# A linear-attention block gated by a mixer: another table of shifts for the scheduler

## The chip, the cores and the metric

The kernel runs on one core of one Trainium2 chip. The metric is the device time of one execution in microseconds (us), the median of the runs. The core has five engines that work from queues of their own: TensorE (PE: matmuls; its weight loads are PEld), VectorE (DVE), ScalarE (ACT), GpSimd (POOL) and SyncE (SP), which here issues transfers. A transfer (DMA) is issued by SP or by POOL; POOL's add to what is already at the destination.

## The reference

```python
def reference(A_x, A_wqkv, A_wo, B_x, B_w1, B_w2, B_w3, B_w4):
    def _A_ref(x, wqkv, wo):
        B, S, D = x.shape
        H = 32; Dh = D // H
        qkv = (lambda x, *d: x.transpose(*d))((x @ wqkv).reshape(B, S, 3, H, Dh), 2, 0, 3, 1, 4)
        q, k, v = qkv[0], qkv[1], qkv[2]
        phi = lambda t: jnp.where(t > 0, t + 1, jnp.exp(t)) + 1e-6
        pq, pk = phi(q), phi(k)
        kv = jnp.einsum("bhsd,bhse->bhde", pk, v)
        z = jnp.einsum("bhsd->bhd", pk)
        num = jnp.einsum("bhqd,bhde->bhqe", pq, kv)
        den = jnp.einsum("bhqd,bhd->bhq", pq, z)[..., None] + 1e-6
        o = num / den
        return (lambda x, *d: x.transpose(*d))(o, 0, 2, 1, 3).reshape(B, S, D) @ wo

    def _B_ref(x, w1, w2, w3, w4):
        h = _gelu(_layernorm(x, axis=-1) @ w1)
...
        hs = jnp.concatenate([g0, g1, g2, g3], axis=-1) @ w2
        x1 = x + hs
        h2 = _gelu(_layernorm(x1, axis=-1) @ w3) @ w4
        return x1 + h2

    x = A_x
    xn = _layernorm(x, axis=-1)
    s = _A_ref(xn, A_wqkv, A_wo)
    g = _silu(_B_ref(xn, B_w1, B_w2, B_w3, B_w4))
    return x + s * g
```

g0 to g3 are the four quarters of h's columns, shifted by +1, -1, +2 and -2 rows. x has 2048 rows of 512 columns, all in f32; the weights are 512 x 1536 (wqkv), 512 x 512 (wo, w1, w2), 512 x 1376 (w3) and 1376 x 512 (w4).

## The kernel before

The rows are worked in sixteen tiles of 128 (i) and four blocks of 512 (b, four tiles each). An f32 operand is split into a high and a low part (names that end in h and l), and a product is made of three matmuls: high by high, low by high, high by low. Many products are further cut into halves on each side and put together from seven smaller products (names s1 to s4 and t1 to t4 are the sums that this takes; a, b, e in pa, pb, pe name the PSUM bank, p1, p5, u2 the partial results that ACT brings out of a bank).

In order of time: the start loads wk and the transposed first block of x (tiles wk_s, xt), splits them into wk_0h, wk_0l and so on and u_0h, u_0l and so on (ACT makes the high parts, DVE the low parts, and DVE sums the weight's chunks into wkt), and makes the keys k. Then come, for all blocks, queries, keys, the 512 x 512 product g of phi(k) and xn, the first mixer product h and the second one; from about 230 us the MLP's first product for block after block (`up_late`), with the attention sums put in between (`attends`: so collects the result, pas, pbs, pes are its banks), and from about 410 us the MLP's second product (`down_late`) for blocks 2, 3 and 1. In `down_late` the results are collected in xo, POOL adds x1 from memory to it by a transfer (xo<-x1d), ACT makes silu of it (th<-xo), DVE multiplies by the attention's result (so, or sb where that comes back from memory), POOL adds x, and SP stores th to out.

Nothing of the order is written out by hand. Each call (`mm`, `act`, `tt`, `stt`, `fetch`, `gather`, ...) only adds an operation to a list, with its engine, an estimate of how long it is busy, and what it reads and writes; the rows of the profile that show L146, L168, L191 and so on are such helpers. `deadlines` (L243) gives each operation a due time, backwards from the time at which PE is expected to need its result. `nudged` (L237) then takes pairs (n, k) from the table and moves the due time of the n-th operation of the list earlier by a quarter of k microseconds (later for a negative k), and `backward` (L279) passes earlier due times on to what feeds it. `emit` (L285) plays all engines forward: it takes for each engine the operations whose inputs are there and for which a buffer is free, and issues of those that can start soonest the one with the earliest due time. So a shift of one due time moves an operation in its engine's queue, and what follows from it in the buffers moves others. Each engine works its queue strictly in the order written here. PSUM has four banks for groups of matmuls (tag mm) and four for the long sums (tag acc): a group can begin when ACT or DVE has read the bank's last content.

The change touches the table `SOONER` (from L1828) alone, in the function that builds the kernel; L1895 hands it to `emit`.

Of the kernel before, what the change touches and what calls it, by code (L numbers as in the profile page):

```python
# [411 lines left out]
def linear_attn_gated_by_mixer(  # L412
# [1401 lines left out]
    for b in LINE:  # L1814
# [14 lines left out]
        25, 43, 34, 17, 48, 11, 52, 22, 57, 4, 63, 3, 76, 3, 88, -164, 90, 14, 91, -77, 94, 30, 95, 2, 96, 3,  # L1829
        97, 30, 98, -40, 100, -16, 103, 30, 105, -42, 112, 38, 115, -66, 118, -34, 124, 73, 125, 16, 129, 1,  # L1830
        147, 3, 150, 6, 151, -80, 176, 20, 207, 16, 216, 3, 233, 11, 234, 29, 248, 17, 252, 3, 259, 25, 261, 42,
        262, 18, 275, 8, 282, -131, 283, -49, 302, 83, 314, -14, 315, 24, 316, 21, 321, 25, 326, 6, 331, 17,
        336, -29, 341, -44, 354, 27, 355, -45, 375, 27, 405, -6, 406, -36, 410, -76, 415, 40, 416, -23, 424, 11,
        427, 23, 428, -30, 433, -9, 434, -77, 435, 22, 443, 67, 445, -24, 451, 7, 454, -24, 456, 18, 478, 13,
        485, -8, 488, -69, 489, -119, 491, -65, 492, -3, 504, 30, 522, 77, 532, -9, 542, -1, 544, 5, 545, 15,
        552, 36, 553, -28, 563, -29, 568, -26, 571, -22, 586, 29, 591, 24, 600, -25, 616, 11, 618, 10, 627, -50,
        631, 22, 650, 6, 654, -53, 657, -29, 660, 9, 676, 8, 678, 7, 688, -19, 694, -22, 704, -15, 705, 19, 710,
        -18, 713, 22, 714, 15, 717, -23, 721, -22, 724, 36, 726, -14, 728, 7, 733, 5, 761, 17, 797, 13, 806, 36,
        807, -10, 814, -15, 815, -38, 827, 85, 844, 20, 847, 3, 849, -51, 862, -35, 867, -36, 870, -19, 873, 31,
        874, -15, 876, -28, 885, 36, 894, 15, 899, 37, 901, -27, 909, 5, 911, 2, 917, 23, 925, 7, 927, -30, 934,  # L1840
        13, 941, -10, 956, -44, 969, 6, 971, -6, 976, -52, 980, -10, 997, 25, 998, -27, 1000, -24, 1005, -17,
        1013, -11, 1024, -19, 1030, -28, 1082, 6, 1087, -28, 1090, -3, 1101, 39, 1103, -27, 1119, 1, 1141, 13,
        1146, 44, 1149, 20, 1153, 9, 1156, 8, 1177, 27, 1179, 67, 1208, -23, 1213, 4, 1227, -38, 1239, -20,
        1262, 21, 1266, 8, 1271, 44, 1277, 35, 1291, 3, 1323, -12, 1324, -6, 1328, -1, 1329, 29, 1330, -16,
        1331, 19, 1333, -8, 1340, -40, 1362, -46, 1367, 18, 1381, 45, 1389, -46, 1399, -12, 1407, 24, 1408, 22,
        1412, 23, 1416, 13, 1419, 24, 1420, -43, 1421, -8, 1436, 8, 1447, 40, 1470, 42, 1474, -49, 1482, 33,
        1489, -12, 1502, -15, 1517, -42, 1521, -8, 1532, -28, 1540, -40, 1563, -18, 1575, 24, 1584, 20, 1588, 8,
        1596, -19, 1613, 37, 1614, 4, 1619, 33, 1620, 15, 1629, -4, 1631, -3, 1641, -35, 1648, 22, 1652, 49,
        1655, 4, 1659, 15, 1661, -4, 1665, -111, 1677, 11, 1679, -11, 1687, -19, 1696, 32, 1699, -20, 1700, 106,
        1703, -55, 1705, -12, 1717, -75, 1724, 10, 1725, 10, 1726, 15, 1741, 12, 1742, 28, 1747, 35, 1749, 12,  # L1850
        1758, 30, 1771, 17, 1779, -149, 1796, -30, 1843, 16, 1845, 18, 1853, -23, 1854, -28, 1855, -4, 1861,
        -22, 1864, 17, 1866, 31, 1881, -67, 1888, -54, 1901, 61, 1925, -37, 1933, -5, 1938, -86, 1943, 43, 1944,
        -6, 1947, 29, 1951, -16, 1955, -38, 1960, -57, 1964, 57, 1972, 19, 1978, 3, 1985, 4, 1990, -28, 1994,
        -42, 1996, -20, 1999, -38, 2000, 20, 2002, -22, 2008, 28, 2011, -25, 2021, 30, 2029, -31, 2048, -15,
        2049, -4, 2050, -3, 2060, 19, 2063, 43, 2067, 12, 2071, 19, 2080, 3, 2084, 22, 2102, 18, 2104, -26,
        2106, -32, 2112, -20, 2119, 24, 2131, -20, 2156, -24, 2158, 7, 2161, -34, 2190, -5, 2213, 12, 2244, 14,
        2258, 2, 2264, 71, 2267, 21, 2270, 19, 2286, -22, 2295, 5, 2298, -50, 2317, 33, 2326, 9, 2340, 14, 2353,
        12, 2357, 31, 2358, -19, 2381, -52, 2382, 1, 2383, 6, 2387, -14, 2389, -27, 2391, -30, 2393, -3, 2394,
        -15, 2406, 32, 2413, 22, 2422, -6, 2423, 26, 2424, -4, 2446, -16, 2452, 2, 2469, 9, 2471, 24, 2476, 31,
        2478, -18, 2482, 16, 2521, -26, 2534, -11, 2543, 24, 2578, -18, 2580, -14, 2585, 21, 2586, -7, 2592, -9,  # L1860
        2610, 16, 2611, 28, 2622, 21, 2626, 6, 2628, -27, 2639, 31, 2644, -22, 2648, 33, 2649, -8, 2656, -13,
        2658, 24, 2672, 29, 2684, -22, 2690, -4, 2691, -19, 2705, -23, 2710, 6, 2718, 6, 2722, -28, 2724, -47,
        2734, 26, 2739, 28, 2751, 44, 2778, 29, 2792, 17, 2804, 3, 2806, -46, 2816, -32, 2822, 20, 2831, -28,
        2833, 13, 2843, 6, 2855, 8, 2859, 52, 2870, 18, 2872, 8, 2875, 17, 2882, 33, 2892, -26, 2895, -23, 2899,
        -32, 2900, 16, 2904, -33, 2907, -13, 2912, 21, 2919, -24, 2926, 10, 2932, 4, 2935, -17, 2936, -40, 2941,
        -40, 2957, -40, 2963, -90, 2966, -48, 2967, -29, 2978, -20, 2980, 30, 2992, 14, 3029, -22, 3032, 9,
        3034, 36, 3055, 30, 3057, -6, 3061, -10, 3072, 62, 3085, 47, 3091, 25, 3094, 8, 3103, 7, 3124, 97, 3140,
        8, 3146, -6, 3156, -16, 3163, 24, 3204, 104, 3210, -44, 3222, -21, 3229, -63, 3239, -51, 3243, -24,
        3274, 55, 3276, 31, 3287, 41, 3288, 25, 3292, 22, 3311, -22, 3314, -18, 3315, -53, 3316, 21, 3319, -77,
        3321, -18, 3327, 2, 3328, -49, 3330, -52, 3347, 12, 3348, 25, 3374, 14, 3380, 18, 3386, 13, 3406, 28,  # L1870
        3407, -30, 3447, -19, 3450, 33, 3454, -46, 3458, 39, 3466, 50, 3469, -18, 3475, -27, 3480, 9, 3484, 35,
        3486, 106, 3490, -26, 3501, -40, 3509, 37, 3516, 10, 3541, 26, 3557, 4, 3559, 5, 3560, 3, 3561, 22,
        3562, 33, 3563, -30, 3570, 17, 3571, 56, 3584, -15, 3608, -28, 3611, 26, 3621, -42, 3626, 4, 3634, -6,
        3646, -38, 3669, 6, 3672, -26, 3676, -26, 3711, -20, 3721, 10, 3723, 5, 3739, 1, 3768, -3, 3776, 2,
        3777, 2, 3783, -4, 3791, -19, 3796, 7, 3813, -17, 3821, 23, 3826, -31, 3829, -38, 3846, -16, 3863, 11,
        3871, 6, 3878, 2, 3882, -23, 3885, -29, 3894, 61, 3897, -18, 3916, -7, 3926, -26, 3974, 6, 3987, 8,
# [59 lines left out]
```

## Time and profile before

| | |
|---|---|
| time, median of 3 runs | 498.81 us (498.80 to 498.99) |
| profiled execution, span | 496.4 us |
| PE busy | 490.6 us, 99% |
| PEld busy | 447.0 us, 90% |
| DVE busy | 438.4 us, 88% |
| ACT busy | 373.4 us, 75% |
| POOL busy | 123.6 us, 25% |
| DMA packets' time, queues of SP and POOL | 59.6% and 24.9% of 16 engines' span |

The span is that of one execution taken by the profiler, from its first to its last instruction; the time of a run has some 2.4 us more around it. The record of a matmul lasts longer than the distance to the next one, so PE's busy share doesn't show a short wait; the distances between the starts do. In a timeline "[0.37 <-DVE u_1l L191]" at a row's end says that the engine was idle for 0.37 us before it, and what ended that.

### The profile page before, as it was taken

What the parts mean: (1) busy time and instruction counts of PE and PEld (TensorE: products, weight loads), DVE (VectorE), ACT (ScalarE), POOL (GpSimd) and SP (SyncE); (2) the same over time, 40 slices, a digit from 0 to 9 for tenths busy, and PEclk for the clock granted to TensorE, in tenths of its full rate; (3) what the DMA queues carried; (4) which work ended last, traced back from release to release, by engine and by line L of the source; (5) the groups of instructions that cost most, each with busy time, mean ns of one, the idle gap of its engine ahead of it and who ended that gap; (6) DMA issues with size and microseconds to landing.
All of it is one profiled execution on the core that took longest, in us unless ns stands there. A gap on an engine that the chain in (4) does not pass through costs nothing.

```text
span 496.4 us, 9885 instructions
## 1 busy us (share of the span) xinstructions
PE 490.6 (99%) x3244; PEld 447.0 (90%) x3244; DVE 438.4 (88%) x874; ACT 373.4 (75%) x845; POOL 123.6 (25%) x214
## 2 busy tenths in 40 slices
PE   8999999999999999999999999999999999999996
PEld 6778888888888999899889999999999999999996
DVE  5998997889989669999999999999999899796864
ACT  5999999677887599999988567765686877565531
POOL 1384404276930232133200021100000000143420
PEclk9999999999999999999999999999999999999999
DMA  7869696999974999999988499984634699599996
GB/s 229 303 187 297 133 296 183 237 287 269 329 220 100 236 310 248 273 252 290 337 268 247 158 194 298 247 262 138 183 114 147 215 336 332 114 226 283 278 224 182
DMA packets 87082, 117.44 MB, mean 237 GB/s; under 512 B 10328, under 2 KB 39160, under 8 KB 87032
## 3 DMA queue, kind: packets, MB, share of 16 engines
q1 hardware_dynamic: 75512, 96.11, 59.6%
q0 software_dynamic: 11520, 20.71, 24.9%
q8 instruction: 25, 0.41, 0.4%
q14 instruction: 25, 0.20, 0.1%
HBM read 72.66 MB, written 39.93 MB: 227 GB/s over the span
## 4 chain that ended last, share of the span: by engine, by line
PE 97%; DMA 1%; SPq 1%; ACT 0%; DVE 0%; issue 0%; ACTq 0%
PE pb L146 12%; PE pbd L146 9%; PE h L146 9%; PE g L146 9%; PE acc L146 6%; PE pe L146 6%; PE pbx L146 6%; PE ped L146 5%; PE pbm L146 5%; PE pbs L146 5%; PE q L146 3%; PE pa L146 3%; PE pex L146 3%; PE k L146 3%; PE pad L146 3%; PE pes L146 2%
## 5 line engine op out<-in xcount | busy, mean ns | idle before, releaser
L225 POOL DMA_DIRECT2D xo<-x1d x12 | 10.9, 950 | 166.2 <-DVE xo L191 118.5
L225 POOL DMA_DIRECT2D th<-in_x x14 | 12.2, 895 | 45.0 <-DVE th L201 23.1
L225 POOL DMA_DIRECT2D o<-xnd x16 | 14.0, 887 | 37.5 <-DVE o L191 13.5
L168 ACT ACTIVATE th<-xo 128x512 f32<-128x512 f32 (+1 forms) x16 | 9.7, 614 | 15.9 <-DVE xo L201 10.1
L225 POOL DMA_DIRECT2D zacc<-ke x12 | 12.9, 1073 | 31.4 <-DMA zacc<-ke 10.4
L191 DVE TENSOR_TENSOR ht<-h,abc 128x512 f32<-128x512 f32 x16 | 11.0, 690 | 7.5 <-PE h L146 7.4
L225 POOL DMA_DIRECT2D xt<-nrow x16 | 14.6, 1288 | 8.4 <-ACT k12h L168 4.1
L196 POOL TENSOR_SCALAR w<-mv 128x4 f32<-128x4 f32 (+2 forms) x10 | 2.5, 254 | 40.7 <-ACT sq L168 40.4
L168 ACT ACTIVATE y<-o,nm,rs 128x512 f32<-128x512 f32 x16 | 12.4, 814 | 0.2 <-POOL nm L196 0.2
L168 ACT ACTIVATE p<-pb 128x256 f32<-128x256 f32 x20 | 7.6, 381 | 5.8 <-PE pb L146 5.4
L168 ACT ACTIVATE ht<-ht 128x512 f32<-128x512 f32 x16 | 10.0, 626 | 2.1 <-DVE ht L191 2.0
L168 ACT ACTIVATE sq<-o,mv 128x512 f32<-128x512 f32 x16 | 11.5, 722 | 0.1
L168 ACT ACTIVATE u<-pb 128x256 f32<-128x256 f32 x20 | 7.7, 383 | 5.1 <-PE pb L146 4.5
L201 DVE SCALAR_TENSOR_TENSOR pq<-pq,rd 128x512 f32<-128x512 f32 x16 | 11.0, 688 | 0.3
L168 ACT ACTIVATE p<-pe 128x256 f32<-128x256 f32 x20 | 7.7, 384 | 4.6 <-PE pe L146 4.1
L201 DVE SCALAR_TENSOR_TENSOR qz<-pq,zb 128x512 f32<-128x512 f32 x16 | 10.8, 682 | 0.0
L1471 DVE TENSOR_REDUCE den<-qz 128x32 f32<-128x512 f32 x16 | 10.8, 679 | 0.0
L168 ACT ACTIVATE sq<-o 128x512 f32<-128x512 f32 x16 | 10.0, 629 | 0.1
L613 POOL TENSOR_TENSOR rs<-w,nhalf 128x4 f32<-128x4 f32 (+2 forms) x10 | 9.7, 970 | 0.8
L168 ACT ACTIVATE x<-x,nm,rs 128x512 f32<-128x512 f32 x12 | 9.2, 805 | 0.0
L201 DVE SCALAR_TENSOR_TENSOR th<-th,so 128x512 f32<-128x512 f32 x12 | 8.2, 683 | 0.6 <-ACT th L168 0.5
L168 ACT ACTIVATE sq<-x,mv 128x512 f32<-128x512 f32 x12 | 8.6, 718 | 0.1
(2075 smaller groups left out, 2446.9 us busy)
## 6 DMA issues: line engine op xcount, KB each, us to landing
w_s<-in_w SPq DMA_DIRECT2D x28, 256.0 KB, 5.6
x<-in_x SPq DMA_DIRECT2D x16, 256.0 KB, 6.2
xt<-in_xt SPq DMA_DIRECT2D x16, 256.0 KB, 6.9
xnd<-x SPq DMA_DIRECT2D x16, 256.0 KB, 5.9
xt<-nrow POOLq DMA_DIRECT2D x16, 256.0 KB, 7.6
pqd<-qr SPq DMA_DIRECT2D x16, 256.0 KB, 6.1
o<-xnd POOLq DMA_DIRECT2D x16, 256.0 KB, 6.6
x1d<-o SPq DMA_DIRECT2D x16, 256.0 KB, 5.1
```

The lines of the kernel that those rows point to most:

```text
L146: lambda: nc.tensor.matmul(out.get(), lhs.get(), rhs.get(), start=start, stop=stop, skip_group_check=more))
L168: nc.scalar.activation(out.get(), src.get(), func, scale=get(scale), **kw)
L191: self.vec(eng, out, [a, b], lambda: self.e(eng).tensor_tensor(out.get(), a.get(), b.get(), op=op), True)
L196: lambda: self.e(eng).tensor_scalar(out.get(), a.get(), get(s1), get(s2), **kw), False,
L201: lambda: self.nc.vector.scalar_tensor_tensor(out.get(), a.get(), get(s), b.get(), op0=op0, op1=op1),
L225: lambda: self.nc.gpsimd.dma_start(out.get(), get(src), accum_op=ALU.add), mb=mb)
L613: lambda: g.tensor_tensor(out.get(), src.get(), nh.get(), op=ALU.pow))
L1471: pl.add("DVE", .6, .68, [t], [den], lambda: nc.vector.tensor_reduce(den.get(), t.get().rearrange("p (h d) -> p h d", d=DH), axis=AX.X, op ...
```

## The change

The table of pairs is replaced by another one with fewer and larger entries. The operations, the list, the planner and its costs are the same. Each engine has the same operations as before, 3219 matmuls, 874 operations on DVE and 786 on ACT among them, in another order, and with other buffers.

```diff
--- before.py
+++ after.py
@@ -1826,71 +1826,56 @@
...
     SOONER = (
-        25, 43, 34, 17, 48, 11, 52, 22, 57, 4, 63, 3, 76, 3, 88, -164, 90, 14, 91, -77, 94, 30, 95, 2, 96, 3,
-        97, 30, 98, -40, 100, -16, 103, 30, 105, -42, 112, 38, 115, -66, 118, -34, 124, 73, 125, 16, 129, 1,
-        147, 3, 150, 6, 151, -80, 176, 20, 207, 16, 216, 3, 233, 11, 234, 29, 248, 17, 252, 3, 259, 25, 261, 42,
...
+        34, 75, 46, 7, 71, 6, 79, -7, 82, -43, 88, -34, 90, 14, 91, -78, 95, 1, 96, 7, 98, -33, 107, 4, 109, 12,
+        113, 8, 115, 46, 116, -144, 125, 13, 137, 11, 147, 2, 151, -30, 154, 12, 156, -14, 166, 14, 182, 19,
+        210, 5, 215, -14, 216, -7, 232, -10, 233, -8, 234, 46, 248, 9, 251, 5, 252, -7, 274, -117, 278, 16, 282,
...
+        5430, 100, 5496, -168, 5536, 41,
     )
     pl.emit(first=6.0, lead={"p": 9.0, "w": 20.0, "ab": 10.0}, reserve={"p": 8, "w": 1, "ab": 0}, window=9.0,
```

At the start, DVE's first operations. Before:

```order
L196 TENSOR_SCALAR wk_0h<-wk_s_100 128x256
L191 TENSOR_TENSOR wk_0l<-wk_s_100,wk_0h 128x512
L191 TENSOR_TENSOR u_0l<-xt_0_106,u_0h 128x256
L191 TENSOR_TENSOR wkt<-wk_s_100,wk_s_118 128x512
L191 TENSOR_TENSOR wk_1l<-wk_s_118,wk_1h 128x512
L191 TENSOR_TENSOR wkt<-wkt,wk_s_122 128x512
L191 TENSOR_TENSOR u_1l<-xt_1_120,u_1h 128x256
L191 TENSOR_TENSOR wk_2l<-wk_s_122,wk_2h 128x512
L191 TENSOR_TENSOR wkt<-wkt,wk_s_128 128x512
L191 TENSOR_TENSOR wk_3l<-wk_s_128,wk_3h 128x512
L191 TENSOR_TENSOR u_2l<-xt_2_124,u_2h 128x256
```

and now:

```order
L196 TENSOR_SCALAR wk_0h<-wk_s_100 128x256
L191 TENSOR_TENSOR wk_0l<-wk_s_100,wk_0h 128x512
L191 TENSOR_TENSOR u_0l<-xt_0_106,u_0h 128x256
L196 TENSOR_SCALAR u_0h<-xt_0_106 128x256
L191 TENSOR_TENSOR u_0l<-xt_0_106,u_0h 128x256
L191 TENSOR_TENSOR wk_1l<-wk_s_118,wk_1h 128x512
L191 TENSOR_TENSOR wkt<-wk_s_100,wk_s_118 128x512
L191 TENSOR_TENSOR wk_2l<-wk_s_122,wk_2h 128x512
L191 TENSOR_TENSOR u_1l<-xt_1_120,u_1h 128x256
L191 TENSOR_TENSOR u_2l<-xt_2_124,u_2h 128x256
L191 TENSOR_TENSOR wkt<-wkt,wk_s_122 128x512
```

The second half of block 0's first chunk (u_0h, u_0l) comes from further down to right behind the first u_0l, and wk_2l stands ahead of u_1l instead of behind it.

PE near 338 us, with attention pair 6 (pes and pbs are two of its banks). Before:

```order
L146 MATMUL pes_4947<-m_t1h,q6s0h 128x256
L146 MATMUL pes_4947<-m_t1l,q6s0h 128x256
L146 MATMUL pes_4947<-m_t1h,q6s0l 128x256
L146 MATMUL pbs_4873<-m_t2h,q6s0l 128x256
L146 MATMUL pbs_4873<-m_t2h,q6s0h 128x256
L146 MATMUL pbs_4873<-m_t2l,q6s0h 128x256
L146 MATMUL pbs_4873<-m_t2h,q6s0l 128x256
L146 MATMUL pes_4947<-m_b22h,q6s1h 128x256
L146 MATMUL pes_4947<-m_b22l,q6s1h 128x256
L146 MATMUL pes_4947<-m_b22h,q6s1l 128x256
L146 MATMUL pes_4947<-m_b22h,q6s1h 128x256
L146 MATMUL pes_4947<-m_b22l,q6s1h 128x256
```

and now:

```order
L146 MATMUL pes_4945<-m_t1h,q6s0h 128x256
L146 MATMUL pes_4945<-m_t1l,q6s0h 128x256
L146 MATMUL pes_4945<-m_t1h,q6s0l 128x256
L146 MATMUL pbs_4920<-m_t2h,q6s0h 128x256
L146 MATMUL pbs_4920<-m_t2l,q6s0h 128x256
L146 MATMUL pbs_4920<-m_t2h,q6s0l 128x256
L146 MATMUL pbs_4920<-m_t2h,q6s0h 128x256
L146 MATMUL pbs_4920<-m_t2l,q6s0h 128x256
L146 MATMUL pbs_4920<-m_t2h,q6s0l 128x256
L146 MATMUL pes_4945<-m_b22h,q6s1h 128x256
L146 MATMUL pes_4945<-m_b22l,q6s1h 128x256
L146 MATMUL pes_4945<-m_b22h,q6s1l 128x256
```

Where four matmuls of pbs stood between the group pes<-m_t1 and the next group in the same bank, pes<-m_b22, six stand now.

DVE in the final block (b = 1), around d_s41l. Before:

```order
L191 TENSOR_TENSOR d1f_s41f<-d1f_s21f,h_ba121f 128x512
L191 TENSOR_TENSOR dl1l<-hl_6876,dl1h 96x512
L191 TENSOR_TENSOR d_s11l<-d1f_s11f,d_s11h 128x512
L201 SCALAR_TENSOR_TENSOR th_7094<-th_7094,so_5785 128x512
L191 TENSOR_TENSOR d_s21l<-d1f_s21f,d_s21h 128x512
L191 TENSOR_TENSOR d_s30l<-d1f_s30f,d_s30h 128x512
L191 TENSOR_TENSOR xo_6629<-pad_7101,p1d_7060 128x256
L191 TENSOR_TENSOR d_a220l<-h_ba220f,d_a220h 128x512
L191 TENSOR_TENSOR p5d_7155<-xo_6844,ped_7084 128x256
L191 TENSOR_TENSOR u2d_7169<-pbd_7034,xo_6629 128x256
L191 TENSOR_TENSOR d_s41l<-d1f_s41f,d_s41h 128x512
```

and now:

```order
L191 TENSOR_TENSOR d_s40l<-d1f_s40f,d_s40h 128x512
L191 TENSOR_TENSOR p5d_7115<-xo_6950,ped_7083 128x256
L201 SCALAR_TENSOR_TENSOR th_7106<-th_7106,so_5783 128x512
L191 TENSOR_TENSOR p1d_7126<-pbd_7059,xo_6806 128x256
L191 TENSOR_TENSOR d_s41l<-d1f_s41f,d_s41h 128x512
L191 TENSOR_TENSOR d_s30l<-d1f_s30f,d_s30h 128x512
L191 TENSOR_TENSOR d_s4xl<-d1f_s4xf,d_s4xh 128x256 x2
L191 TENSOR_TENSOR d_s31l<-d1f_s31f,d_s31h 128x512
```

Before, the difference p1d (of banks pbd and xo) stands two rows above the first of these, so that eleven operations, the th among them, lie between it and d_s41l. Now th comes ahead of p1d, and d_s41l directly behind.

## Rows read from the trace of the kernel before

**Rows 1.** The page: head, part 1, and the chain that ended last.

```profile
span 496.4 us, 9885 instructions
...
PE 490.6 (99%) x3244; PEld 447.0 (90%) x3244; DVE 438.4 (88%) x874; ACT 373.4 (75%) x845; POOL 123.6 (25%) x214
...
PE 97%; DMA 1%; SPq 1%; ACT 0%; DVE 0%; issue 0%; ACTq 0%
```

**Rows 2.** Stretches: from:to, length; busy (instructions) PE, PEld, DVE, ACT, POOL; clock; DMA; GB/s.

```profile
230.00:290.00 60.00, 60.00 (x386) 54.08 (x385) 59.17 (x117) 50.12 (x119) 6.58 (x11) 1.00 0.81 251
290.00:350.00 60.00, 59.93 (x502) 59.59 (x501) 59.44 (x125) 40.83 (x106) 5.19 (x6) 1.00 0.88 235
```

**Rows 3.** PE's waits: engine, line, waited for; us in total, times, longest.

```profile
PE k L146 <- DVE u_1l L191: 0.4, 1, 0.4
```

**Rows 4.** Timeline 6.5 to 14: start, us, engine, line, operation, out<-in, shapes, [idle before].

```profile
7.36 0.41 ACT L168 ACTIVATE u_1h<-xt 128x256 fp32r<-128x256 f32 x1
7.49 0.69 DVE L191 TENSOR_TENSOR wk_1l<-wk_s,wk_1h 128x512 fp32r<-128x512 f32 x1
...
8.50 0.64 ACT L168 ACTIVATE wk_2h<-wk_s 128x512 fp32r<-128x512 f32 x1 [0.74 <-DMA wk_s<-in_wqkv]
8.57 0.69 DVE L191 TENSOR_TENSOR wkt<-wkt,wk_s 128x512 f32<-128x512 f32 x1 [0.40 <-DMA wk_s<-in_wqkv]
...
8.90 0.39 PE L146 MATMUL k<-wk_1l,u_1h 128*128 128x512 f32 x1
...
9.18 0.42 DVE L191 TENSOR_TENSOR u_1l<-xt,u_1h 128x256 fp32r<-128x256 f32 x1
...
9.66 0.51 PE L146 MATMUL k<-wk_1h,u_1l 128*128 128x512 f32 x1 [0.37 <-DVE u_1l L191]
...
10.00 0.40 PE L146 MATMUL k<-wk_2h,u_2h 128*128 128x512 f32 x1
...
10.23 0.40 PE L146 MATMUL k<-wk_1h,u_1h 128*128 128x512 f32 x1
```

**Rows 5.** Timeline around 338 us, same columns: PE and ACT at bank pes.

```profile
337.77 0.28 PE L146 MATMUL pes<-m_t1h,q6s0l 128*128 128x256 f32 x1
...
338.15 0.39 ACT L168 ACTIVATE p5s<-pes 128x256 f32<-128x256 f32 x1 [1.16 <-PE pes L146]
338.24 0.28 PE L146 MATMUL pbs<-m_t2h,q6s0l 128*128 128x256 f32 x1
...
338.59 0.39 PE L146 MATMUL pes<-m_b22h,q6s1h 128*128 128x256 f32 x1
...
338.81 0.28 PE L146 MATMUL pes<-m_b22l,q6s1h 128*128 128x256 f32 x1
```

**Rows 6.** Timeline around 357 us, same columns.

```profile
357.15 0.42 DVE L191 TENSOR_TENSOR so<-pbs,p5s 128x256 f32<-128x256 f32 x1
...
357.63 0.39 PE L146 MATMUL pbs<-m_t4h,q 128*128 128x256 f32 x1
```

**Rows 7.** Timeline around 383 us, same columns.

```profile
383.16 0.39 DVE L191 TENSOR_TENSOR h_a220f<-pb,p 128x256 f32<-128x256 f32 x1
...
383.60 0.38 PE L146 MATMUL pb<-yt43h,w_b 128*128 128x256 f32 x1
```

**Rows 8.** Final block: timelines of three engines; issues 445 to 465 (count, KB, us to landing).

```profile
464.75 0.42 DVE L191 TENSOR_TENSOR p1d<-pbd,xo 128x256 f32<-128x256 f32 x1 [0.73 <-PE pbd L146]
...
473.86 0.69 DVE L191 TENSOR_TENSOR d_s41l<-d1f_s41f,d_s41h 128x512 fp32r<-128x512 f32 x1 [1.81 <-PE pbd L146]
...
454.60 0.86 POOL L225 DMA_DIRECT2D xo<-x1d  x1 [3.47 <-DVE xo L191]
...
466.57 0.63 ACT L168 ACTIVATE th<-xo 128x512 f32<-128x512 f32 x1
...
xo<-x1d POOLq DMA_DIRECT2D x2, 256.0 KB, 7.5
...
d1f_s30f<-hd POOLq DMA_DIRECT2D x1, 256.0 KB, 11.4
```

108 rows, old and new, of the table SOONER are left out of this document.

## The prediction

> **What bounds the kernel now.** The page comes first: TensorE (PE) is busy 490.6 of a span of 496.4 us, and the chain that ended last is PE for 97% [rows 1]. A table that only re-orders can't take matmuls out, so all it can give is time in which PE stood still, and all it can cost is more of that. The table by stretches says where such time can be: PE is busy in all of each stretch but the first 10 us and the tail, and VectorE (DVE) is busy 59.17 and 59.44 of 60 us from 230 to 350 [rows 2]; there a late result of DVE has no slack to hide in. The view of the engine's waits names one real wait, PE for u_1l, 0.4 us [rows 3]. Busy time hides short waits, because the record of a matmul is longer than the distance to the next one (0.28 us long, 0.118 us apart for 256 columns). So I went through the starts of PE's matmuls from the timeline and took each distance beyond the usual one. What I found: 0.63 us at the start, 0.34 us at 338.6, 0.18 us at 357.6, 0.10 us at 383.8, 0.07 us at 321.5, and about 0.4 us in some five shorter ones. That is 1.7 us, and no order of the same operations gains more than this. The run's median is 498.81 us, the profiled span 496.4, so 2.4 us lie around the span; I take them as fixed.
>
> **The change, part by part.** Nothing is added or removed: each engine has the same operations. Only the order, and with it buffers and waits, differs.
>
> *The start: a loss of about 0.14 us.* In the kernel before, PE issues k<-wk_1l,u_1h at 8.90; the next would come 0.23 us later, at 9.13, but it wants u_1l, which DVE makes at 9.18 (0.42 us) behind a wkt that came at 8.57 because wk_s2 landed then. PE goes on at 9.66, and the next start is 0.34 us behind it in place of 0.23 (10.00, then 10.23): 0.53 + 0.11, in all 0.63 us [rows 4]. In the new order two more 512-column matmuls (0.47 us) stand in front of the first use of u_1l, so PE would come to it at 9.60. But DVE now makes wk_2l before u_1l, and wk_2l needs wk_2h, which ACT has at 9.14 (8.50 and 0.64). So wk_2l goes at 9.17, and u_1l 0.60 us later (the distance between 8.57 and 9.18), at 9.77 with 0.42 to run; PE goes on at 10.25, with the 0.11 us of restart 10.36. On the way PE meets two more operands with no time left: u_1h ends at 7.77 and is wanted at 7.81 (about 0.13 us with the weight load that nothing covers), and wk_1l ends at 8.18 and is wanted at 8.17 (0.18 us) [rows 4]. So PE wants u_1l at 9.91, waits 0.45, and the start costs 0.13 + 0.18 + 0.45, some 0.77 us against 0.63: **+0.14**. Bounds: 0 if the two near misses are hits (the last wait only grows by what they save, so little is saved), +0.5 if wk_s2 lands half a microsecond later, on which both orders hang.
>
> The Trainium skill (VectorE: DVE Perf Modes, section "The DRAIN you can't avoid") says that the next DVE operation doesn't start until the pipe has run empty; by that u_1l would come 0.09 us later, at a full 0.69 us, and this term would be +0.23. The trace differs: at 8.57 and 9.18 the distance is 0.61 beside a duration of 0.69 [rows 4].
>
> *338.6: a gain of 0.34 us.* PE ends a group in bank pes at a start of 337.77, ACT evicts it as p5s at 338.15 (0.39), and PE uses the bank again at 338.59. Only four matmuls of pbs lie between; the fourth starts at 338.24, so the bank was wanted at 338.36: 0.23 us, and 0.11 more of restart (338.81 after 338.59) [rows 5]. It is the one place with fewer than six matmuls between eviction and reuse. In the new order all six of pbs stand there. The bank is then wanted at 337.77 + 7 x 0.118 = 338.60, and comes at 338.59: the wait is gone, without a margin. Ten places before have six matmuls and no wait there, which is why I take the whole **-0.34**; bounds -0.34 and -0.1.
>
> *357.6: a gain of 0.18 us.* PE wanted pbs again and waited for DVE's so (357.15, 0.42 us), which stood behind a scaling of pq [rows 6]. In the new order so follows another so directly and seven matmuls lie between its release and the reuse; by counting it ends at 357.85 and is wanted at 358.2. **-0.18.** *383.8: a gain of 0.10 us.* h_a220f at 383.16 (0.39 us) stood behind a transpose, and PE, which was ready for the next group a few hundredths earlier, started it at 383.60 and lost the rest in the restart [rows 7]. Now the release comes two matmuls earlier and eight lie between: slack 0.4 us. **-0.10.**
>
> *New near misses: a loss of about 0.3 us.* The new order has eleven places with six matmuls of cover, and several that had nine or ten now have seven (the attention sums so of the last pairs, near 390 and 404 us). By the durations of before four or five of them have a slack of 0 with an error of 0.2 us either way. Each that fails costs 0.11 us of restart and the miss itself. I take one wait of the 338.6 kind, +0.3; bounds 0 and five of them, 1.7.
>
> *The tail: 0.* After PE's last matmul an ACT, two DVE operations and a store follow; the new order has the same ones in the same order.
>
> Sum: -0.34 - 0.18 - 0.10 + 0.14 + 0.3 = **-0.18 us**: a span of 496.2 and a time of **498.6 us**.
>
> **The rivals.** *All waits go (faster).* If the near misses hold, the sum is -0.48; if the restarts of the shorter waits go too (-0.47), -0.95, about 497.9; with the start's 0.63 gone as well 497.2. For it: every real wait of before but the start has more cover now. Against it: the start's order puts u_1l later, and I find nothing that removes the wait for wk_s2. Time: 497.1 to 497.8.
>
> *A late landing in the final block (slower).* Before, DVE makes p1d at 464.75 and d_s41l at 473.86 [rows 8]. In the new order its sequence is th (times so), p1d, d_s41l, and PE wants d_s41l at 470.0. That th needs ACT's th, and this the landing of the gather into xo, which POOL can issue only when DVE has xo: 454.60 before [rows 8], and 30 matmuls later now, 458.1. A landing after 7.5 us, as the two xo of that stretch before, gives 465.6 (ACT's th before started at 466.57 [rows 8]). The way from there is 0.63 (ACT) + 0.69 + 0.42 + 0.69 (DVE), 2.3 us with overlaps and hand-offs, so d_s41l comes by 467.9; p1d itself waits for PE until 468.4 and then sets 469.5: slack 0.5 us. It decides from a landing longer than 9.5 us. The gather of d1f_s30f beside it took 11.4 [rows 8]: then d_s41l comes at 471.9 and PE stands 1.9 us, **500.5 us**. For it: in this stretch the transfers share the DMA engines with the outputs. Against it: both xo gathers took 7.5.
>
> *DVE falls behind between 230 and 400 us (slower).* DVE has under 1 us of idle time in each 60 there [rows 2], so a result that comes late stays late for its followers. By counting, its lead over PE changes by at most 0.7 us between the two orders, which the covers of seven and more take. If it doesn't: lost hand-offs at 0.34 each; from four on the sum is above +0.8 and the time 499.8 to 501.
>
> *The table does nothing.* Then the waits of before would all be there and the time 498.8. The order of instructions speaks against it: DVE differs from its third operation on.
>
> **How the numbers follow.** 0.2%, about what a measurement of this kernel can tell from no change, is 1.0 us. The forecast (some waits gone, some new, within 1 us) has 0.66, with a range of its own of 497.8 to 499.8; all waits gone 0.14; late landing 0.08; DVE behind 0.10; nothing changed 0.02. Same is 0.66 + 0.02 = 0.68, faster 0.14, slower 0.18. The low end, 497.7, is reached by the sum with every wait but the start's gone (-1.1); the high end, 500.0, by +0.14, -0.62 and the upper bound of the near misses, 1.7 (+1.2). Below 497.7 lies some 0.1, above 500.0 some 0.1.
>
> **What would show it.** The timeline of the changed kernel should have no distance over 0.25 us at 338.6, at 357.6 and 383.8, where before had one; PE's first wait for DVE should again be u_1l, ending at about 10.2; the wait of u_1h or wk_1l just before it should be under 0.2 us. The forecast is wrong if PE stands longer than 1 us in all between 230 and 410 (DVE behind), if PE waits at 470 for d_s41l (late landing), or if the start's wait is under 0.3 us.

## The result, and the profile after

The changed kernel takes 500.38 us (median of 15 runs, 498.50 to 503.27), the kernel before beside it 498.52 us (15 runs, 498.08 to 499.16). The ratio is 1.0039, with an interval from 1.0026 to 1.0052: **slower by 0.4%**, 1.9 us. The forecast was 498.6 us with a range up to 500.0, so the result lies outside it, on the side that had 18 in 100. Two things stand in these numbers: the loss, and a spread of almost 5 us where the kernel before spreads over 1.

The page of the changed kernel, answering to [rows 1] (its run took 501.07 us, 0.7 above the median):

```profile
span 499.4 us, 9892 instructions
...
PE 490.8 (98%) x3244; PEld 445.8 (89%) x3244; DVE 438.5 (88%) x874; ACT 372.9 (75%) x845; POOL 125.4 (25%) x214
...
PE 91%; DMA 5%; DVE 1%; SPq 1%; ACT 1%; issue 1%; DVEq 0%; ACTq 0%; POOLq 0%
```

The busy times are within 2 us of those of before. The chain tells more: PE held 97% of it, now 91%, and 5% are transfers. The table by stretches says where (from:to, length; busy time and instructions of PE, PEld, DVE, ACT, POOL; clock; DMA share; GB/s). First the changed kernel:

```profile
130.00:180.00 50.00, 48.66 (x255) 41.21 (x254) 42.77 (x87) 36.94 (x78) 13.80 (x30) 1.00 0.82 222
180.00:230.00 50.00, 49.14 (x349) 45.81 (x348) 44.42 (x97) 46.69 (x116) 13.28 (x18) 1.00 0.94 246
230.00:290.00 60.00, 60.00 (x396) 54.76 (x395) 58.56 (x116) 49.91 (x124) 5.95 (x10) 1.00 0.83 260
290.00:350.00 60.00, 60.00 (x491) 59.05 (x490) 59.59 (x123) 40.92 (x106) 7.01 (x8) 1.00 0.87 237
```

Then two stretches of the kernel before, which the prediction did not use:

```profile
130.00:180.00 50.00, 50.00 (x262) 42.55 (x262) 41.29 (x86) 37.02 (x79) 16.05 (x36) 1.00 0.79 210
180.00:230.00 50.00, 50.00 (x367) 47.32 (x366) 46.41 (x98) 48.74 (x124) 14.48 (x20) 1.00 1.02 276
```

From 230 on, where the prediction looked (compare [rows 2]), PE has no gap that this view shows. From 130 to 230, where before had none, it stands for 1.34 and 0.86 us. The view of the engine's waits names what it stood for (us in total, times, longest):

```profile
PE pbm L146 <- ACT u2m L168: 1.3, 1, 1.3
...
PE pem L146 <- ACT p5m L168: 0.9, 1, 0.9
PE k L146 <- ACT u_1h L168: 0.8, 1, 0.8
PE k L146 <- DVE u_1l L191: 0.5, 1, 0.5
```

Adding up what each distance between the starts of two matmuls has beyond the usual one (0.233 us for 512 columns, 0.118 for 256) gives the whole account of this profile: 11.81 us against 8.51 in the kernel before (matmuls of 128 columns, the same in both, are in both totals; only the difference is read). Of the 3.30 us more, 0.80 come before 25 us, 2.65 between 150 and 200, -0.19 between 325 and 400, and 0.04 from the rest.

**The first new place**, 172.75 us, in timelines of PE, ACT and POOL of the changed kernel (start, us, engine, line, operation, out<-in, shapes, [idle before <-releaser]):

```profile
171.02 0.39 PE L146 MATMUL h<-u_1h,w_1h 128*128 128x512 f32 x1
172.75 0.39 PE L146 MATMUL pbm<-w_t3h,hs30h 128*128 128x256 f32 x1 [1.34 <-ACT u2m L168]
...
171.70 0.63 ACT L168 ACTIVATE sq<-o 128x512 f32<-128x512 f32 x1 [3.06 <-DMA o<-xnd]
...
172.33 0.36 ACT L168 ACTIVATE u2m<-pbm 128x256 f32<-128x256 f32 x1
...
165.00 1.76 POOL L225 DMA_DIRECT2D o<-xnd  x2 [13.34 <-DMA wv_s<-in_wqkv]
```

PE wants the bank pbm, which ACT frees by the eviction u2m. But ACT's queue holds, ahead of u2m, the sum of squares of another tile (sq<-o, for the norm behind the mixer). That one needs the tile with the residual added, and the residual comes by a transfer that POOL issues from 165.00 on. ACT stands 3.06 us for its landing, u2m, which doesn't need it, stands behind it, and PE stands 1.34 us and loses another 0.26 in the pace around it.

**The second**, 186.41 us, is built alike, with p5m as the eviction and another tile's transfer:

```profile
184.49 1.05 PE L146 MATMUL kv<-gs,wv_s 128*128 128x128 f32 x8
186.41 0.39 PE L146 MATMUL pem<-w_b22h,hs41h 128*128 128x256 f32 x1 [0.86 <-ACT p5m L168]
...
184.52 0.63 ACT L168 ACTIVATE sq<-o 128x512 f32<-128x512 f32 x1 [2.65 <-DMA o<-xnd]
...
185.99 0.36 ACT L168 ACTIVATE p5m<-pem 128x256 f32<-128x256 f32 x1
...
177.48 0.88 POOL L225 DMA_DIRECT2D o<-xnd  x1 [2.25 <-ACT o L168]
```

In the kernel before the same statistics stand behind these evictions, u2m and p5m (ACT, then POOL):

```profile
169.62 0.39 ACT L168 ACTIVATE u2m<-pbm 128x256 f32<-128x256 f32 x1 [1.92 <-PE pbm L146]
...
174.10 0.63 ACT L168 ACTIVATE sq<-o 128x512 f32<-128x512 f32 x1
...
181.48 0.39 ACT L168 ACTIVATE p5m<-pem 128x256 f32<-128x256 f32 x1
182.00 0.63 ACT L168 ACTIVATE sq<-o 128x512 f32<-128x512 f32 x1
...
164.21 1.77 POOL L225 DMA_DIRECT2D o<-xnd  x2 [10.08 <-DVE hs2f L191]
...
174.50 0.86 POOL L225 DMA_DIRECT2D o<-xnd  x1 [2.88 <-PE h L146]
```

So the old order gives the first landing 9.9 us (164.21 to 174.10) before ACT comes to it, and the second 7.5 (174.50 to 182.00). In the new one ACT is there 3.6 us after the issue (171.70 - 3.06 - 165.00) and 4.4 us after it (184.52 - 2.65 - 177.48). The landing itself was not quicker in the old order: there the first transfer took 8.9 us, in the new one 6.7.

### The profile page after: what moved, and what is told of

Read it like the earlier page. It is cut to its first block, busy times and chain, and to the rows that moved or that the text cites. A ratio compares the mean times of both kernels' runs of the same rounds, so it can differ in the third digit from the quotient of the medians.

```text
span 499.4 us, 9892 instructions
## 1 busy us (share of the span) xinstructions
PE 490.8 (98%) x3244; PEld 445.8 (89%) x3244; DVE 438.5 (88%) x874; ACT 372.9 (75%) x845; POOL 125.4 (25%) x214
## 4 chain that ended last, share of the span: by engine, by line
PE 91%; DMA 5%; DVE 1%; SPq 1%; ACT 1%; issue 1%; DVEq 0%; ACTq 0%; POOLq 0%
PE pb L146 11%; PE pbd L146 9%; PE g L146 9%; PE acc L146 6%; PE h L146 6%; PE pe L146 6%; PE pbx L146 6%; PE ped L146 5%; PE pbs L146 5%; PE pbm L146 3%; PE q L146 3%; PE pa L146 3%; PE pex L146 3%; DMA o<-xnd 3%; PE k L146 3%; PE pad L146 3%
```

## The experiments

Two explanations stood against each other: that the two landings in ScalarE's queue make the loss, and that the start does (its 0.80 us, and what follows from it). In all kernels below the planner's order is made first and then operations are moved in it; nothing else differs unless it is said. The diffs show rows of an engine's queue. Ratios are to the kernel before, run beside each.

**One statistic put back.** Only sq of the first tile moves, on ScalarE's queue of the changed kernel:

```diff
-sq <- o (tile 0)
 u2m <- pbm
+sq <- o (tile 0)
```

> The changed kernel with one ACT operation moved: the first statistic of tile 0 in the second mixer product (sq<-o, which needs the landing of POOL's gather o<-xnd) goes behind the eviction u2m of bank pbm instead of in front of it. Theory (a statistic that waits for a landing stands in ACT's queue ahead of an eviction that PE waits for): PE's wait at 172.7 us, 1.5 us and 0.1 us of restart in the profile of the changed kernel, is gone, the second one at 186.4 stays; the median falls from 500.4 to about 499.3, ratio to before near 1.0015 to 1.002. Rival (the start alone makes the difference, and waits behind it are given back later): the wait goes, but the median stays within 0.3 us of 500.4.

Measured: 502.07 us (6 runs), ratio 1.0074 [1.0060, 1.0088], slower than the changed kernel's 1.0039. The wait at 172.7 is gone, and the next one has grown (ACT, then PE):

```profile
184.31 0.63 ACT L168 ACTIVATE sq<-o 128x512 f32<-128x512 f32 x1 [4.40 <-DMA o<-xnd]
...
186.20 0.38 PE L146 MATMUL pem<-w_b22h,hs41h 128*128 128x256 f32 x1 [2.72 <-ACT p5m L168]
```

Neither the expected 499.3 us with the second wait unchanged nor its rival came. PE came to the second place earlier and waited there for a transfer that was issued 1.6 us earlier than in the changed kernel (175.87 against 177.48) and let ACT go on only 0.2 us earlier (184.31 against 184.52). So the wait taken out in front of this landing was not gained.

That the kernel is even slower than the changed one comes from the clock. Behind the stop of 2.72 us the granted clock fell to the 1.2 GHz level (stretch 187 to 190.5):

```profile
187.00:190.50 3.50, 3.50 (x19) 3.50 (x18) 2.07 (x5) 3.06 (x5) 2.17 (x4) 0.51 0.22 50
```

At 0.51 over 3.5 us this is some 1.7 us lost. Five of the six runs have a mean clock of 0.997 and take 501.9 to 502.8 us; the sixth has 0.999 and takes 499.81.

**Both put back**, sq of tile 0 behind u2m and both statistics of tile 3, with POOL's w, behind p5m and u2m.

> The changed kernel with both statistics moved: sq<-o of tile 0 behind u2m at 172.7 us, and the two sq<-o of tile 3 behind p5m and u2m at 186.4 us (with them the POOL operation w that reads their sums). Theory: no PE wait over 0.3 us between 130 and 230; median about 498.6 (500.4 less the two waits, of which a typical run has somewhat less than the 2.7 us of the profiled one), ratio 0.999 to 1.001, and the spread of the runs (498.5 to 503.3 in the changed kernel) shrinks to under 2 us, because both waits hang on landings. Rival (start alone): 499.8 or more, spread as before.

Measured: 499.55 us (5 runs), 1.0039 [1.0026, 1.0052]. Both waits are gone and a third stands behind them (DVE, then PE):

```profile
188.24 0.71 DVE L155 STREAM_TRANSPOSE y_1z<-y 128x512 f32<-128x512 f32 x1 [0.98 <-ACT y L168]
...
189.06 0.41 DVE L191 TENSOR_TENSOR o<-pbm,p5m 128x256 f32<-128x256 f32 x1
...
189.52 0.39 PE L146 MATMUL pbm<-w_t4h,ha221h 128*128 128x256 f32 x1 [1.27 <-DVE o L191]
```

This is the same chain one step on: sq feeds POOL's pow, pow the scale of the normalised y on ACT, y its transpose on DVE, and the new table has that transpose ahead of the eviction o. But in this profile it is no longer the landing that is late. It came 6.3 us after the issue at 175.38, so by 181.7, and the statistic, which I had put behind u2m too, where the kernel before has it between p5m and u2m, begins 1.4 us later without having waited (its row shows no idle time):

```profile
183.13 0.63 ACT L168 ACTIVATE sq<-o 128x512 f32<-128x512 f32 x1
```

So the third wait belongs at least in part to my own move. The expectation of 498.6 us missed, though both waits went.

**The chain moved link by link.** Three moves (the transpose behind o as well), four (the three y behind the eviction p1m, their transposes later), five (one y and its transpose behind the next u2m); three and four also with the first 98 operations in the order of the kernel before.

```diff
 three:  VectorE   -transpose y_1z    o <- pbm,p5m    +transpose y_1z
 four:   ScalarE   -y, y, y           p1m <- pbm      +y   kvrh   o <- pbm   +y, y
 five:   ScalarE   -y (tile 0)        u2m <- pbm      +y (tile 0)
```

> The changed kernel with three moves: both statistics behind the evictions as in the run with two moves, and DVE's o<-pbm,p5m of the same product ahead of the transpose y_1z (with the store of that transpose), which waits for the statistics' result by way of POOL and ACT. Theory: the 1.3 us wait that came up at 189.5 us when both statistics were moved is gone as well; PE stands under 0.3 us between 140 and 200; median 498.3 to 499.0. Rival (PE is tied to the landing in still another way): a wait of about the same size at a next place, median 499.3 or more.

> The same three moves and the order of the kernel before in the first 98 operations. Theory: the sum of both repairs; median 497.7 to 498.4, at or a little under before (gains of 0.3 to 0.6 us in the later part), spread under 1.5 us. If it stays above 498.8, something in the new order besides the start and the mixer stage costs time (late landings in the final block).

> The changed kernel with the statistics of tiles 0 and 3 behind u2m and behind the last eviction before them, as before, and now also the three normalisations y on ScalarE and their transposes on VectorE behind p1m, the eviction that TensorE waited 1.5 us for in the run with three moves. Theory A, the chain of hand-offs is short and ends here: no wait over 0.3 us between 150 and 200 us, and a time like that of the run without the two gathers, 497.7 to 498.4 us. Theory B, the queue hands the wait on as long as the gathers land 7 us after their issue: another wait of 1 to 2 us between 189 and 197 us, on an eviction or on kvrl or kvrh that now stands behind a y or a transpose, and 499.5 to 500.7 us.

> The same with the first 98 operations in the order of the kernel before. Theory A: as the run above less 0.5 to 0.8 us for the start, 497.2 to 497.9 us, below both kernels. Theory B: 499.0 to 500.0 us, with the same wait near 190 us as in the run above.

> The changed kernel with the four moves and a fifth, the normalisation y of tile 0 with its transpose behind the eviction u2m that TensorE waited 1.1 us for at 192.9 us. One y of 0.8 us less stands ahead of u2m. Theory A, the wait is the sum of the y's in front of the eviction: 0.3 us are left of it, and 499.7 to 500.1 us. Theory B, the wait is set by something else on the chain (the landing, the pow on GpSimd): 1 us stays there or shows up at the next eviction before 200 us, and 500.3 to 501.0 us.

Measured: 1.0042 [1.0029, 1.0055] with three, 1.0026 [1.0017, 1.0036] with the old start; 1.0051 [1.0032, 1.0070] with four, 1.0035 [1.0023, 1.0048] with the old start; 1.0026 [1.0016, 1.0035] with five, 499.78 us. PE's longest wait of this stage in the profile with three, then with four, then the two that are left with five:

```profile
PE pbm L146 <- ACT p1m L168: 1.5, 1, 1.5
```

```profile
PE pbm L146 <- ACT u2m L168: 1.1, 1, 1.1
```

```profile
PE m L146 <- ACT kvrh L168: 0.3, 1, 0.3
PE pbm L146 <- ACT u2m L168: 0.3, 1, 0.3
```

The wait walks down the chain from 186 to 189.5, 191.3 and 192.9 us and shrinks only when the last link has moved; the readings that three or four moves end it fell. In the run with four, three y in a row (2.37 us, ending at 192.6) stood ahead of u2m, and taking one out left 0.3 of 1.1 us, which is its 0.8. The loss is not gone with it: by the distances between the starts, 180 to 200 us holds 1.5 us more with five moves than in the kernel before, now in several short waits and the slow pace behind each. None of these versions reaches the kernel before.

**The landings taken away.** The changed kernel without the two transfers, o<-xnd of tiles 0 and 3; the residual of these two tiles is left out (1509 and 1570 are the two operations' numbers). The same from the kernel before as a control, and from the changed kernel with the old start.

```diff
+    SKIP = 1509, 1570
...
-            op.emit()
+            if op.order not in self.SKIP:
+                op.emit()
```

> The changed kernel, in its own order, without two transfers: the gathers that add xn to o of tiles 0 and 3 in the second mixer product (so the residual is missing in x1 of these two tiles). The statistics sq<-o stay where they are, ahead of u2m and of p5m, but have no landing to wait for. Theory (PE's waits at 172.7 and 186.4 are waits for these two landings, handed on through ACT's queue): both waits are gone, PE stands under 0.3 us between 140 and 230, the median falls by 1.3 to 2.2 us to 498.2 to 499.1, and the spread of the runs becomes that of the start alone, under 2 us. Rival (ACT itself is late there, by its order): waits of over 0.5 us stay at one of the two places, median 499.8 or more.

> The kernel before, without the gathers that add the residual of tiles 0 and 3 in the second product (left out, as in the run on the changed kernel). Theory A, the two landings cost the kernel before nothing, since its statistics stand behind the evictions: 498.2 to 498.7 us, no difference from the kernel before, and no wait between 150 and 200 us in either. Theory B, leaving the two gathers out relieves the DMA queues and gains time anywhere: 497.7 to 498.1 us, and then part of the gain of the changed kernel without them is not the waits.

> The changed kernel without the residual of tiles 0 and 3 in the second product (its two gathers are left out), and with the first 98 operations in the order of the kernel before. What the start costs stands then by itself, with no landing to cover it. Theory A, the new start costs 0.5 to 0.8 us: 497.2 to 497.5 us against 497.99 of the run with the new start, and waits for u_1h gone. Theory B, the start's loss is given back in the next stage, where x0h and the weights' landings set the pace: 497.8 to 498.1 us.

Measured: the changed kernel without them 497.99 us (11 runs, 497.66 to 498.70), 0.9988 [0.9979, 0.9997]; the kernel before without them 498.27 us, 0.9992 [0.9983, 1.0001]; with the old start 497.95 us, 0.9993 [0.9984, 1.0001]. The changed kernel without the transfers, by stretches:

```profile
130.00:180.00 50.00, 50.00 (x264) 42.69 (x263) 42.92 (x88) 38.41 (x82) 11.82 (x28) 1.00 0.80 226
180.00:230.00 50.00, 50.00 (x362) 47.02 (x361) 46.84 (x102) 48.01 (x120) 13.63 (x19) 1.00 0.93 245
```

PE has no gap any more in these stretches, and the spread falls from 4.8 to 1.0 us. The two transfers cost the changed kernel 1.0039 - 0.9988, 0.5% or 2.5 us, and the kernel before 0.08%, 0.4 us, which its interval doesn't tell from nothing. What is left of the table without them, 0.9988 against 0.9992, is 0.2 us in its favour and within the error.

**The other way round.** The kernel before, with sq of tile 0 ahead of u2m:

```diff
+sq <- o (tile 0)
 u2m <- pbm
-sq <- o (tile 0)
```

> The kernel before with one ACT operation moved the other way: sq<-o of tile 0 ahead of the eviction u2m of bank pbm near 169.6 us (it stood five operations behind it). Theory: PE waits there for u2m until the gather o<-xnd has landed, some 1 to 2 us after the eviction was possible (issue at 164.2, landing 6.7 to 8 us later, eviction before at 169.6); median 499.3 to 500.3, ratio 1.0015 to 1.0035, and the spread of the runs grows beyond the 1.1 us of before. Rival (such a wait is given back later): ratio within 0.001 of 1.

Measured: 504.14 us (4 runs), 1.0121 [1.0108, 1.0134]. One operation out of place makes 6 us (ACT, then PE, then stretch 175 to 180):

```profile
173.62 0.63 ACT L168 ACTIVATE sq<-o 128x512 f32<-128x512 f32 x1 [5.55 <-DMA o<-xnd]
...
174.66 0.38 PE L146 MATMUL pbm<-w_t3h,hs30h 128*128 128x256 f32 x1 [3.79 <-ACT u2m L168]
...
176.16 0.63 PE L146 MATMUL h<-u_2h,w_2h 128*128 128x512 f32 x1
176.59 0.63 PE L146 MATMUL h<-u_2l,w_2h 128*128 128x512 f32 x1
...
175.00:180.00 5.00, 5.00 (x22) 4.31 (x21) 1.08 (x3) 0.87 (x3) 0.86 (x1) 0.66 0.79 208
```

The transfer issued at 164.57 was there 9.0 us later. PE stood 3.8 us, and behind that the granted clock fell: two matmuls of 512 columns start 0.43 us apart in place of 0.233, and the mean of that stretch is 0.66. That is some 1.7 us lost (5 us times 0.34), and with the stop it makes most of the 6 us. Expected were 499.3 to 500.3 us: the landing was assumed at 6.7 to 8 us, and the clock was not thought of.

**The start.** The changed kernel with the first 98 operations in the order of before, and the kernel before with the first 96 in the order of the changed one.

> The changed kernel with the order of the kernel before in the first 98 operations (about the first 14 us), everything behind it unchanged. If the new start is slower by its order, as the forecast had it (+0.14 us): the median falls by 0.1 to 0.3 us, to about 500.2. If it is slower by the 0.8 us of the profiled run: to about 499.6. If that was a late landing of wk_s1 and wk_s2 in one run: unchanged, 500.4. The waits at 172.7 and 186.4 stay, so the ratio to before stays at 1.002 or more.

> The kernel before with the new order of the first 96 operations (about 14 us). The forecast's step: +0.14 us, median 498.2 to 498.3. If the new start is worse than its working had it: +0.5 to +0.8 us, 498.6 to 498.9, as the change the other way round (the changed kernel with the old start: 0.6 us less) suggests. PE's waits for u_1h and u_1l at about 8 and 10.4 us are then 0.7 to 1.5 us together in the profile, against 0.63 us before.

Measured: 499.77 us, 1.0040 [1.0027, 1.0052], no better than the changed kernel; and 499.40 us, 1.0020 [1.0011, 1.0029], slower than before by 1.0 us. In the second there is no wait for u_1l, but one at the seam to the old order, where neither of the two whole orders has one:

```profile
19.95 0.73 PE L146 MATMUL g<-k0h,x0h 128*128 128x512 f32 x2 [0.69 <-ACT x0h L168]
```

With the landings out of the way (497.99 against 497.95 us, above) the two starts are worth the same within the error, so the loss is not the start's. The pairs don't all agree, though: with three and with four moves the old start is 0.8 us better (1.0026 against 1.0042, 1.0035 against 1.0051), with intervals that overlap. What the start's order costs by itself is not settled.

**Whole stages exchanged.** Operations planned between 140 and 200 us (in the second kernel, from the start to 200 us) in the order of the other kernel, with buffers dealt anew:

> The changed kernel with the order of the kernel before for all operations that the plan places between 140 and 200 us (the second mixer product of block 0 and the products between), everything else in the new order; buffers are given out anew in the order that results. Theory now (in this stage the new order puts PE, ACT and DVE so close behind the landings of the gathers o<-xnd that a wait which is taken away at one place comes back at the next): no PE wait over 0.3 us between 140 and 200, median 498.3 to 498.9, spread of the runs under 1.5 us; what is left over before is the start. Rival (the loss sits in the start and is spread over the rest, the stage only shows it): the median stays at 499.5 or more.

> The changed kernel with the order of the kernel before from the start to 200 us in the plan, and the new order behind it. Theory: with start and stage gone only the gains of the later part are left (338.6, 357.6, 383.8: 0.6 us less about 0.4 us of new near misses), so the median is 497.7 to 498.1, ratio 0.999 to 1.000. If the later part of the new order loses as well (the final block's late landings), it stays above 498.6.

> The kernel before with the new order for all operations that the plan places between 140 and 200 us, everything else as before. Theory: the waits of PE for u2m and p5m near 170 and 184 us appear, 0.5 to 3 us together from run to run; median 499.3 to 500.3, ratio 1.0025 to 1.0045, spread over 1.5 us. Rival: median within 0.4 us of before.

Measured: 1.0058 [1.0044, 1.0072], 1.0068 [1.0056, 1.0081] and 1.0192 [1.0170, 1.0213]. The first two have no wait between 160 and 190, but new ones where the orders meet (pam<-DVE ht, 0.8 and 0.3 us). The third has the wait for u2m (1.5 us), beside 2.9 us at its seam. None came out as expected, and for the size of the loss they tell nothing, since the seams cost as much.

**A version made from the readings.** The kernel before with two edits: u_1l ahead of the second wkt, and the two matmuls of pbs that 338.6 us lacked.

> The kernel before with three operations moved, as its own trace suggests: DVE's u_1l ahead of the second wkt at the start (it waited behind it for wk_s2, which it doesn't need), and the two early matmuls of pbs<-m_t2 of attention pair 6 behind the group pes<-m_t1, so that six instead of four matmuls cover the eviction at 338.6 us. Theory (order of waits): the wait of 0.5 to 0.6 us for u_1l and the one of 0.34 us are gone; median 0.7 to 1.0 us under before, 497.4 to 497.7, ratio 0.998 to 0.9986. If the start's gain is given back (PE meets wk_2h or u_2l next), ratio 0.999 to 1.

Measured: 498.11 us, 0.9993 [0.9984, 1.0002]: not told from the kernel before, where a gain of 0.7 to 1.0 us was expected. At 338 us only the restart is left, 0.1 us, but 0.11 and 0.08 us of the same kind have come at 335.9 and 337.4; at the start the wait for u_1l is gone and one of 0.4 us for u_2h has come.

## Why the prediction was wrong

**The step that failed is the sum's list of places.** I read waits, starts and orders at the places where the kernel before had lost time, and in the stretches from 230 on because DVE is full there [rows 2]. Between the start and 230 us nothing stood in the sum. An order that is new from DVE's fourth operation on (the prediction says the third, but the first three are the same) can lose time where the old one lost none. None of the three signs that were to show the forecast wrong came either: PE stands some 0.6 us in all between 230 and 410 (distances of 0.05 and more), not 1, it has no wait at 470, and the start's wait is not under 0.3 us. All three looked elsewhere. The term that is missing is 2.65 us of the profiled execution and about 2 us of the medians (2.5 against 0.4).

**It could have been priced from the old trace and the new order.** This row of the kernel before, from the page's part on transfers, was there:

```profile
o<-xnd POOLq DMA_DIRECT2D x16, 256.0 KB, 6.6
```

The places are taken here from the trace of the changed kernel; ahead of the result they would have to be counted from the new queues, as I did for u_1l. In the new order PE wants pbm at 171.25, sq and u2m take about 1 us from 171.70 to the release, so the landing may take at most 5.2 us from 165.00; for the second, by the same count (186.41 - 1.03, less 1.47 from sq to p5m and 0.42 to the release, is 183.5), 6.0 us from 177.48. Against 6.6 us that is 1.4 and 0.6, some 2 us, which is what the medians show. That it fits so well is in part luck: 6.6 is the median of sixteen transfers, and these two took 8.9 and 7.4 us in the kernel before, by which the loss would be 3.7 and 1.4. Either price puts the time above the range. By the planner's own figures in the code the two transfers take 4.8 and 6.0 us, and its plan lets each statistic start 0.06 us behind its landing; with these the plan ends at 495.6 us, with the old table at 496.4. The table gained in the plan what it lost on the chip.

**The right mechanism stood at the wrong place.** A late landing was a rival with 8 in 100, for xo in the final block. There it didn't come: the changed kernel has no wait of PE at d_s41l. That its 500.5 us stands next to the measured 500.38 is chance. I had not asked which other operations of the new order stand behind a landing with less time than before.

**The steps that held.** 338.6 (-0.34): what is left of it in the changed kernel is 0.09 us of restart, answering to [rows 5]:

```profile
342.14 0.37 PE L146 MATMUL pes<-m_b22h,q6s1h 128*128 128x256 f32 x1
342.35 0.28 PE L146 MATMUL pes<-m_b22l,q6s1h 128*128 128x256 f32 x1
```

So -0.25, within its bounds; "without a margin" was right. The 0.18 us of [rows 6] and the 0.10 of [rows 7] are gone. New near misses: 0.10 at 326.5, 0.19 at 338.5, 0.10 at 381.1, some 0.4 us against 0.3. The tail: 0 up to the last store, which took 0.3 us less in this execution.

**The start** was forecast at +0.14 with bounds 0 and +0.5, and shows +0.80 in this execution, answering to [rows 4] (ACT, PE, DVE of the changed kernel):

```profile
7.03 0.63 ACT L168 ACTIVATE wk_1h<-wk_s 128x512 fp32r<-128x512 f32 x1 [1.72 <-DMA wk_s<-in_wqkv]
...
9.03 0.63 ACT L168 ACTIVATE wk_2h<-wk_s 128x512 fp32r<-128x512 f32 x1 [1.06 <-DMA wk_s<-in_wqkv]
...
8.02 0.49 PE L146 MATMUL k<-wk_1h,u_1h 128*128 128x512 f32 x1 [0.83 <-ACT u_1h L168]
...
10.78 0.73 PE L146 MATMUL k<-wk_1h,u_1l 128*128 128x512 f32 x2 [0.51 <-DVE u_1l L191]
...
9.69 0.69 DVE L191 TENSOR_TENSOR wk_2l<-wk_s,wk_2h 128x512 fp32r<-128x512 f32 x1 [0.70 <-ACT wk_2h L168]
10.30 0.42 DVE L191 TENSOR_TENSOR u_1l<-xt,u_1h 128x256 fp32r<-128x256 f32 x1
```

The order of the steps is the one forecast: u_1h missed, then wk_2l ahead of u_1l, then the wait. The sizes differ since wk_s2 landed 0.53 us later than before (9.03 against 8.50) and u_1h was missed by 0.83 instead of 0.13, where the prediction wanted under 0.2; PE goes on with u_1l at 10.78, not at 10.2. In the profiles of all kernels PE's waits in the start sum to 0.3 to 1.3 us with the new order (0.3 with three moves, 1.3 here) and to 0.3 to 1.4 with the old one (0.4 in [rows 3], 1.4 in the kernel before without the two transfers). The two ranges are the same, so most of the size is one execution's landings. In the medians the term is nought in two pairs and 0.8 us in two others, as said above; +0.14 is neither shown nor refuted. The distance of 9.69 and 10.30 is 0.61 us beside a duration of 0.69 again. The section of the Trainium skill that the prediction had weighed (VectorE: DVE Perf Modes, section "The DRAIN you can't avoid") says itself that a next operation which is not held starts earlier; these rows fit that, and the +0.23 by the full duration did not come.

**The two bases.** I put 2.4 us around the span, from a span of one execution and a median of three runs. The changed kernel's own pair gives 1.7 (501.07 and 499.4). This shifts nothing in a difference, but the sum should have stood against a time of its own execution. One rival has a slip as well: with the start's 0.63 gone its sum is 497.1, as in its own range, and not 497.2.

What the prediction had apart from the missing term, -0.18 us, is near to what the two kernels without the landings show, -0.2 us, though both are below what the runs can tell from zero. One thing stays open: how much of the 0.4 us that leaving out the transfers gains in the kernel before is a wait, and how much lighter traffic.

## What to carry to other kernels

When an order is replaced, list for each in-order engine the operations that need a transfer, and compare two times for each: from the issue to where the engine comes to it in the new order, and what such a transfer takes in the trace. Where the first is shorter, whatever stands behind it in the queue is late, and an eviction there stops TensorE. A wait on such a chain is not repaired at one link: the next link has been ordered for the same lateness. And an order that a planner found with landings shorter than the real ones is to be suspected wherever it puts an operation right behind one: here 4.8 and 6.0 us were planned and 6.7 and 7.0 came.

## What had not been expected of the hardware

The same transfer of 256 KB (tile 0's o<-xnd, issued by POOL between 164.0 and 165.2 us) took 5.6 us (164.03 to 169.63, the kernel with the old start) to 7.2 us in the kernels with the new order of this stage, and 8.6 to 9.0 us in those with the old one (8.9 in the kernel before, 9.0 with sq in front). So its time hangs on the order around it, by more than the whole difference between the kernels; what in the order does it is not shown. Each kernel has one trace, so how much it varies from execution to execution isn't shown either. That the changed kernel's spread comes by way of the two transfers is shown, since it falls to 1.0 us without them.

A stop of TensorE can cost more than itself. Behind the stops of 2.72 us (one statistic put back), 2.93 us (the third exchanged stage) and 3.79 us (sq in front) the granted clock went to the 1.2 GHz level for a while, each time some 1.7 us lost; behind those of 1.34 and 0.86 us in the changed kernel's trace it stayed at 1.00 in the rows above. In the slowest run of the changed kernel, 503.27 us, the mean clock is 0.996, in the other fourteen 0.998 to 1.000: that run probably holds such a stretch too, but it has no trace.
